# Causal attention with a gated layer and a soft mixture on one core: the score tiles of a pair's step in another order

## Chip, cores and metric

The kernel runs on one core of a Trainium2 chip. The metric is the time on the device in microseconds (us), the median over runs of the same program. The profiled execution has a time of its own and is shown beside it.

## What is computed

Three layers in a chain, the output of each being the input of the next:

```python
# attention: 4 batches x 12 heads, seq 448, head_dim 64, causal
scores = scale * q @ k.T                      # masked above the diagonal
scores = scores - scores.max(-1)
attn   = exp(scores) / (exp(scores).sum(-1) + 1e-9)
x      = attn @ v                             # -> (1792 tokens, 768)
# layer
h = x @ w_in                                  # 768 -> 2048
x = np.maximum(0.01 * h, h) @ w_out           # 2048 -> 768
# soft mixture: 8 experts, 4 slots each
logits = x @ phi                              # (1792, 32)
d = softmax(logits, over tokens); c = softmax(logits, over slots)
slot_input = d.T @ x
slot_out   = for each expert: relu(slot_input @ w1) @ w2
out = c @ slot_out
```

## The kernel before

**Tiling.** Two heads make a pair; there are 24 pairs, n = 0 to 23, six to a batch (`NP`). For each pair a step is written, in three slots, by the generator `attention_slots` (L517). Its first loop covers n = 0 to 6 and is not touched; its second loop (L563 on) covers n = 7 to 24. While a pair is attended, the score maxima of the next pair are made: a step holds the work of the pairs n - 1, n and n + 1.

**What a step makes.** The names are those of the trace; every TensorE instruction has the line of the helper that chains them, L102.
- `maxima(n + 1, tiles)` writes one or two of the four row blocks of raw scores into a tile S (block 3 is 448 columns wide, block 2 is 336, block 1 is 224, block 0 is 112, each for two heads). VectorE reads each block and head with one reduction (`junk<-S`, L372) and a short readout of 0.08 us, which give the row maxima `mxe`. `TILES` = ((3,), (0, 2), (1,)) names the three S tiles: S3, S02, S1.
- `lowering(n)` transposes the maxima (`mps`), and ScalarE spreads them into `mr` (L384).
- `weights(n, g)`, g = 0, 1, 2, writes the transposed scores minus the maxima into a tile T (T0, T1, T2; widths 448, 336, and 224 beside 112), which ScalarE turns into exponentials `P` (`P<-T`, L408). GpSimd masks and sums them (L412, L417, L421).
- `attend` multiplies `P` with v into `O`; `inverses` sums the denominators (`dn`), which ScalarE copies (L448) and VectorE inverts in two instructions (`rs`, L450); `columns` scales `O` (VectorE L483, ScalarE L484, GpSimd L485); `qk_stacks` transposes q and k of a later pair (`qkps`), read by ScalarE L349 and VectorE L350.

**The ring.** S and T tiles share one tag of two PSUM buffers and take them in turn. So each S or T tile waits for the reader of the tile two before it: VectorE's reductions if that is an S, ScalarE's exponential if it is a T.

**The rest of the work.** `stage` walks the slots. After each slot of attention TensorE gets one column of x @ w_in of the batch before: 18 matmuls into one buffer H (`up`), read by ScalarE (`g`, L669). Two of a batch's 18 slots have no column (`GAPS = (6, 15)`): the first slots of the steps n = 9, 12, 15, 18 and 21. Between these come conversions of w_in to a pair of 16-bit halves: ScalarE L200, L201, L221, L228, VectorE L203 to L205, GpSimd L222; and from about 270 us on those of w_out, with transposes `wt_ps` and products `wp_ps` on TensorE.

**Order.** TensorE's instructions are chained one after the other in the order in which the code writes them (`in_order`). On the other engines a scheduler sets the order, with attention and H ahead of conversions by a priority. Step n = 7 begins at 116.8 us, step 13 at 246.4 us, the last S tile is made in step 22, and attention ends at 502 us. What follows is H of the last batch, the logits and the experts.

Of the kernel before, what the change touches and what calls it, by code (L numbers as in the profile page):

```python
# [34 lines left out]
def tile_attn_moe_softmoe(ctx: ExitStack, tc: tile.TileContext, q, k, v, w_in, w_out, phi, w1, w2, out, dbg=None):  # L35
# [268 lines left out]
    def load_qk(n):  # L304
        b, hp = divmod(n, NP)
        t = att.tile([CP, 2, 2 * NI * D], F32, tag="qk", bufs=2, name=f"qk{n}")
        t = t.rearrange("p j (c x) -> p j c x", c=NI)
        for j, src in enumerate((q, k)):
            for a in range(2):
                nc.sync.dma_start(  # L310
                    t[:, j, :, D * a : D * (a + 1)], src[b, 2 * hp + a].rearrange("(c p) d -> p c d", p=CP)
                )
        qk_t[n] = t
        loaded_last()
# [11 lines left out]
    def reduce_v(n):  # L326

        b, hp = divmod(n, NP)
        if hp == 0:
            v_am[b] = am = const.tile([128, NP + 1], F32, tag="v_am", bufs=2, name=f"v_am{b}")  # L330
            nc.vector.memset(am, 0.0)
        with tc.issue_after(last_on(mybir.EngineType.DVE)) if b else ExitStack():
            nc.vector.tensor_reduce(v_am[b][:CP, hp : hp + 1], v_t[n], AX.XY, ALU.max, apply_absolute_value=True)

    def v_scale(b):

        am = v_am[b]
        nc.vector.tensor_reduce(am[:, NP:], am[:, :NP], AX.X, ALU.max)
        s_v[b], inv_v[b] = pow2_scale(am[:, NP:], f"v{b}")

    def qk_stacks(n):

        t = qk_t.pop(n)
        st = att.tile([128, 2, 2, S], F32R, tag="qs", bufs=2, name=f"qkt{n}")
        for j in range(2):
            p = ps_tr(f"qkps{n}_{j}", (128, S))
            for c in range(NI):
                tr(p[:, CP * c : CP * (c + 1)], t[:, j, c], ident[:CP, :CP])
            nc.scalar.copy(st[:, j, 0], p)  # L349
            nc.vector.tensor_tensor(st[:, j, 1], p, st[:, j, 0].bitcast(F32), ALU.subtract)  # L350
        st_t[n] = st

    def maxima(n, tiles):

        st = st_t[n]
        ps = psum.tile([CP, 2, 512], F32, tag="S", bufs=2, name=f"S{n}_{tiles[0]}")
        at = 0
        for i in tiles:
            w = CP * (i + 1)
            for a in range(2):  # L360
                r = slice(64 * a, 64 * a + 64)
                mm(
                    ps[:, a, at : at + w], st[r, 0, 0, CP * i : w], st[r, 1, 0, :w], start=True, stop=True,
                    skip_group_check=True,
                )
            at += w
        at = 0
        for i in tiles:
            w = CP * (i + 1)
            for a in range(2):  # L370
                junk = att.tile([CP, S], BF16, tag="junk", bufs=1, name=f"junk{n}_{i}_{a}")
                nc.vector.tensor_tensor_reduce(  # L372
                    out=junk[:, :w], in0=ps[:, a, at : at + w], in1=mask[:, S - w :], scale=-1.0, scalar=3e38,
                    op0=ALU.add, op1=ALU.min, accum_out=mxe[n % 2][:, 64 * a + i : 64 * a + i + 1],
                )
            at += w
# [9 lines left out]
    def weights(n, g):  # L386

        st, mr = st_t[n], mr_t[n].rearrange("p i c -> p (i c)")
        p = pbuf[n % 2]
        ps = psum.tile([CP, 2, 512], F32, tag="S", bufs=2, name=f"T{n}_{g}")  # L390
        at = 0
        for j in ((0,), (1,), (2, 3))[g]:
            w = S - CP * j
            for step, (kh, qh) in enumerate(((0, 0), (1, 0), (0, 1), (None, None))):
                for a in range(2):
                    r = slice(64 * a, 64 * a + 64)
                    dst = ps[:, a, at : at + w]
                    if kh is None:
                        mm(dst, onesr[r], mr[r, CP * j :], start=False, stop=True, skip_group_check=True)
                    else:  # L400
                        mm(
                            dst, st[r, 1, kh, CP * j : CP * (j + 1)], st[r, 0, qh, CP * j :], start=step == 0, stop=False,
                            skip_group_check=True,
                        )
            at += w
        x = p[g // 2][:CP].rearrange("p a j c -> p a (j c)")
        o = S if g == 1 else 0
        nc.scalar.activation(x[:, :, o : o + at], ps[:, :, :at], AF.Exp, scale=SCALE)  # L408
        if g:

            d = p[g // 2][:CP].rearrange("p a j c -> p (a j) c")[..., :CP]
            nc.gpsimd.affine_select(  # L412
                out=d, in_=d, compare_op=ALU.is_ge, fill=0.0, base=0, pattern=[[0, 4], [1, CP]], channel_multiplier=-1,
            )

        if g == 1:
            nc.gpsimd.tensor_tensor(tsum[:CP], p[0][:CP, :, 0, CP:], p[0][:CP, :, 1, : S - CP], ALU.add)  # L417
        if g == 2:
            for j in range(2):
                y = tsum[:CP, :, CP * (j + 1) :]  # L420
                nc.gpsimd.tensor_tensor(y, y, p[1][:CP, :, j, : S - CP * (j + 2)], ALU.add)  # L421
            del st_t[n], mr_t[n]
# [4 lines left out]
    def attend(n):  # L427

        p, vt = pbuf[n % 2], v_t.pop(n)
        o_t[n] = o = psum.tile([128, S], F32, tag="O", name=f"O{n}")  # L430
        for j in range(NI):
            for a in range(2):
                mm(
                    o[64 * a : 64 * a + 64, CP * j :], vt[:, a * NI + j, :], p[j // 2][:CP, a, j % 2, : S - CP * j],
                    start=j == 0, stop=j == NI - 1, skip_group_check=True,
                )
# [80 lines left out]
    def attention_slots():  # L517


        for n in range(2):  # L520
            qk_stacks(n)
            load_qk(n + 2)
            if n == 0:
                for tiles in TILES:
                    maxima(0, tiles)
        for x in range(NP):
            reduce_v(x)
        v_scale(0)
        for n in range(NP + 1):
            here, more = n < NPAIR, n + 1 < NPAIR  # L530
            if n > 0:
                attend(n - 1)
            if here:
                lowering(n)
            if more:
                maxima(n + 1, TILES[0])
            if here:
                weights(n, 0)
            yield
            if n > 0:  # L540
                inverses(n - 1)
            if more:
                maxima(n + 1, TILES[1])
            if here:
                weights(n, 1)
            yield
            if n > 0:
                columns(n - 1)
            if here:
                weights(n, 2)  # L550
            if more:
                maxima(n + 1, TILES[2])
            if n + 2 < NPAIR:
                qk_stacks(n + 2)
                if n + 4 < NPAIR:
                    load_qk(n + 4)
            if n + NP < NPAIR:
                load_v(n + NP)
            if NP <= n + NP - 1 < NPAIR:
                reduce_v(n + NP - 1)  # L560
            yield

        for n in range(NP + 1, NPAIR + 1):  # L563
            here, more = n < NPAIR, n + 1 < NPAIR
            attend(n - 1)
            inverses(n - 1)
            if here:
                lowering(n)
            yield
            if more:  # L570
                maxima(n + 1, TILES[0])
            if here:
                weights(n, 0)
            if n % NP == 1 and n + NP - 2 < NPAIR:
                v_scale(n // NP)
            yield
            columns(n - 1)
            if here:
                weights(n, 1)
            if more:  # L580
                maxima(n + 1, TILES[1])
            if here:
                weights(n, 2)
            if more:
                maxima(n + 1, TILES[2])
            if n + 2 < NPAIR:
                qk_stacks(n + 2)
                if n + 4 < NPAIR:
                    load_qk(n + 4)
            if n + NP < NPAIR:  # L590
                load_v(n + NP)
            if n + NP - 1 < NPAIR:
                reduce_v(n + NP - 1)
            yield

    TILES = ((3,), (0, 2), (1,))
    slots_of_attention = attention_slots()


# [484 lines left out]
```

## Time and profile before

| | us |
|---|---|
| median of 3 runs (lowest, highest) | 722.96 (722.45, 725.35) |
| profiled execution: its time | 725.07 |
| profiled execution: span, first to last instruction | 723.3 |
| TensorE busy in it | 603.6 (83%) |
| VectorE, ScalarE, GpSimd busy | 360.0, 290.9, 232.7 |
[...]

The profiled execution lies 2.11 us above the median. Working with its rows gives a time against 725.07; 2.11 less gives one against the median. A row of the timeline is start, duration, engine, line, operation, what it writes and reads, and in brackets how long its engine stood idle before it, with what ended that. A matmul row groups neighbouring matmuls of one shape; their ends are modelled.

### The profile page before, as it was taken

How to read it: one execution, taken by the hardware profiler on the slowest of the kernel's cores; microseconds unless marked ns; L12 is line 12 of the kernel's file. 1: busy time of each engine (PE TensorE's matmuls, PEld its weight loads, DVE VectorE, ACT ScalarE, POOL GpSimd, SP SyncE). 2: the span in 40 equal slices, each digit the busy share in tenths (PEclk: the TensorE clock that was granted, in tenths of full speed). 3: DMA queues.
4: the chain of work that ended last, by engine and by line, in shares of the span. 5: the costliest groups of instructions: out<-in, count | busy, mean ns of one | idle time of the engine just before them, and what ended most of it. 6: DMA issues, size and time to landing. Idle time of an engine off the chain costs nothing.

```text
span 723.3 us, 12309 instructions
## 1 busy us (share of the span) xinstructions
PE 603.6 (83%) x4836; PEld 342.0 (47%) x4836; DVE 360.0 (50%) x884; ACT 290.9 (40%) x571; POOL 232.7 (32%) x247
## 2 busy tenths in 40 slices
PE   3788858879889988898988978899998996998464
PEld 2465634555545545555555545454443443453124
DVE  5878646578775554464446446543646423101004
ACT  1677543466863444554435334442121112011003
POOL 4368742476763344243333233322000000000000
PEclk9999998899999988999998989999999998899968
DMA  9933163353642364463422311303989436999957
GB/s 197 251 87 77 39 188 90 108 157 90 189 145 64 105 176 139 127 185 96 108 77 79 88 47 62 93 24 118 328 318 357 157 106 241 424 423 424 424 237 305
DMA packets 102449, 125.67 MB, mean 174 GB/s; under 512 B 69240, under 2 KB 91256, under 8 KB 98296
## 3 DMA queue, kind: packets, MB, share of 16 engines
q1 hardware_dynamic: 102392, 124.89, 52.3%
q8 instruction: 38, 0.62, 0.4%
q14 instruction: 19, 0.16, 0.1%
HBM read 105.74 MB, written 19.14 MB: 173 GB/s over the span
## 4 chain that ended last, share of the span: by engine, by line
PE 52%; DVE 14%; DMA 13%; ACT 8%; POOL 6%; issue 4%; SPq 1%; DVEq 0%; ACTq 0%; POOLq 0%
PE H L102 25%; DMA w<-in_moe_w_dram 8%; PE O L102 4%; DVE junk L372 3%; PE T L102 3%; DMA raw_i_None<-in_moe_w_in_dram 3%; PE g_acc L102 3%; PE qkps L102 2%; DVE g_nat L609 2%; PE ph L942 2%; PE dn L102 2%; PE L L102 2%; DVE cv_i_None L205 2%; PE S L102 2%; POOL cv_i_None L222 2%
## 5 line engine op out<-in xcount | busy, mean ns | idle before, releaser
L102 PE MATMUL H<-x,w 128*128 128x448 f16 x1152 | 243.5, 368 | 2.1 <-ACT g L669 2.1
L102 PEld LDWEIGHTS <-w 128*128 128x128 f16 x1152 | 115.5, 103 | 122.3 <-issue 35.4
L372 DVE CUSTOM_DVE_ANT_0 junk<-S,mask 112x448 bf16<-112x448 f32 (+1 forms) x192 | 85.2, 444 | 51.2 <-PE S L102 47.7
L669 ACT ACTIVATE g<-H,iv 128x448 f32<-128x448 f32 x58 | 36.7, 632 | 120.0 <-PE H L102 104.3
L102 PE MATMUL T<-qkt 64*112 64x336 f32 (+3 forms) x576 | 60.8, 323 | 26.6 <-ACT P L408 25.9
L450 DVE RECIPROCAL rs<-rs 128x224 f32<-128x224 f32 x36 | 53.4, 1524 | 38.5 <-ACT rs L448 38.5
L408 ACT ACTIVATE P<-T 112x672 f32<-112x672 f32 (+1 forms) x72 | 56.9, 790 | 29.3 <-PE T L102 29.1
L102 PEld LDWEIGHTS T<-qkt 64*112 64x112 f32 x576 | 44.0, 183 | 37.2 <-ACT P L408 30.0
L102 PE MATMUL O<-P,v 112*64 112x448 f32 (+3 forms) x384 | 55.3, 429 | 6.3 <-POOL P L412 4.0
L412 POOL TENSOR_SCALAR_AFFINE_SELECT P<-P 112x448 f32<-112x448 f32 x48 | 31.3, 653 | 76.9 <-ACT P L408 74.2
L485 POOL TENSOR_TENSOR x<-rs,x 128x448 f16<-128x448 f32 x24 | 25.7, 1071 | 85.3 <-ACT x L484 79.9
L102 PE MATMUL S<-qkt 64*112 64x448 f32 (+1 forms) x192 | 32.6, 380 | 17.3 <-DVE mxe L372 13.7
L421 POOL TENSOR_TENSOR tsum<-tsum,P 112x448 f32<-112x448 f32 (+1 forms) x48 | 44.3, 922 | 3.3
L1030 PE MATMUL po<-w,hz 128*32 128x384 f32 x256 | 27.9, 557 | 19.1 <-DMA w<-in_moe_w_dram 19.1
L102 PEld LDWEIGHTS O<-P,v 112*64 112x64 f32 x384 | 26.5, 143 | 34.3 <-issue 16.4
L417 POOL TENSOR_TENSOR tsum<-P 112x672 f32<-112x672 f32 x24 | 40.1, 1670 | 1.5
L609 DVE STREAM_TRANSPOSE g_nat<-g 128x448 f32<-128x448 f32 x26 | 16.5, 639 | 44.0 <-ACT g L669 44.0
L350 DVE TENSOR_TENSOR qkt<-qkps,qkt 128x448 fp32r<-128x448 f32 x48 | 28.4, 619 | 18.0 <-ACT qkt L349 17.5
L934 POOL MEMSET hz<- 128x256 f32 x2 | 0.6, 311 | 108.5 <-PE g_acc L102 108.5
L102 PE MATMUL qkps<-ident,qk 112*128 112x112 f32 x192 | 31.6, 323 | 4.3 <-DMA qk<-in_q_dram 4.3
L222 POOL TENSOR_TENSOR cv_i_None<-cv_i_None,cs_i_None 128x768 f32<-128x768 f32 x16 | 26.3, 1647 | 23.7 <-ACT cs_i_None L221 23.7
L102 PE MATMUL T<-mr,onesr 64*112 64x448 f32 (+1 forms) x192 | 31.2, 321 | 2.4 <-ACT mr L384 2.4
(174 smaller groups left out, 855.7 us busy)
## 6 DMA issues: line engine op xcount, KB each, us to landing
w<-in_moe_w_dram SPq DMA_DIRECT2D x32, 1536.0 KB, 20.5
raw_i_None<-in_moe_w_in_dram SPq DMA_DIRECT2D x16, 768.0 KB, 4.8
raw_o_None<-in_moe_w_out_dram SPq DMA_DIRECT2D x10, 768.0 KB, 6.0
g_far<-g SPq DMA_DIRECT2D x32, 224.0 KB, 6.9
gb<-g_far SPq DMA_DIRECT2D x8, 896.0 KB, 6.8
wo<-wsc SPq DMA_DIRECT2D x4, 1536.0 KB, 9.7
qk<-in_q_dram SPq DMA_DIRECT2D x48, 112.0 KB, 2.4
qk<-in_k_dram SPq DMA_DIRECT2D x48, 112.0 KB, 2.7
```

The lines of the kernel that those rows point to most:

```text
L102: op(*args, **kwargs)
L222: nc.gpsimd.tensor_tensor(t, t, sg, ALU.mult)
L350: nc.vector.tensor_tensor(st[:, j, 1], p, st[:, j, 0].bitcast(F32), ALU.subtract)
L372: nc.vector.tensor_tensor_reduce(out=junk[:, :w], in0=ps[:, a, at : at + w], in1=mask[:, S - w :], scale=-1.0, scalar=3e38, op0=ALU.add, o ...
L408: nc.scalar.activation(x[:, :, o : o + at], ps[:, :, :at], AF.Exp, scale=SCALE)
L412: nc.gpsimd.affine_select(out=d, in_=d, compare_op=ALU.is_ge, fill=0.0, base=0, pattern=[[0, 4], [1, CP]], channel_multiplier=-1,)
L417: nc.gpsimd.tensor_tensor(tsum[:CP], p[0][:CP, :, 0, CP:], p[0][:CP, :, 1, : S - CP], ALU.add)
L421: nc.gpsimd.tensor_tensor(y, y, p[1][:CP, :, j, : S - CP * (j + 2)], ALU.add)
L450: nc.vector.reciprocal(rs[:, c : c + S // 2], rs[:, c : c + S // 2])
L609: nc.vector.transpose(g_nat[:, :, 32 * f : 32 * (f + n)].rearrange("p c (f x) -> p f c x", x=32), gts[b, f].rearrange("p (c x) -> p c x", ...
L669: nc.scalar.activation(g, ps, AF.Prelu, scale=iv[b][:, f : f + 1], alpha=SLOPE)
L1030: nc.tensor.matmul(po[h][32 * g : 32 * g + 32], hp[:, (t0 + t) % 8], wt[:, t, DH * h - c0 : DH * (h + 1) - c0], start=t0 + t < 4, stop=t0 ...
```

## The change

The second loop writes the same tiles in another order. Slot 2 held S3, T0 and now holds S1, T0, S3. Slot 3 held T1, S02, T2, S1 and now holds T1, T2, S02. Nothing is added or removed.

```diff
--- before.py
+++ after.py
@@ -568,21 +568,20 @@
                 lowering(n)
             yield
             if more:
-                maxima(n + 1, TILES[0])
+                maxima(n + 1, TILES[2])
             if here:
                 weights(n, 0)
+            if more:
+                maxima(n + 1, TILES[0])
             if n % NP == 1 and n + NP - 2 < NPAIR:
                 v_scale(n // NP)
             yield
             columns(n - 1)
             if here:
                 weights(n, 1)
+                weights(n, 2)
             if more:
                 maxima(n + 1, TILES[1])
-            if here:
-                weights(n, 2)
-            if more:
-                maxima(n + 1, TILES[2])
             if n + 2 < NPAIR:
                 qk_stacks(n + 2)
                 if n + 4 < NPAIR:
```

With A and B for the two buffers, and in brackets whose reader a tile waits for:
- before: S3 A (T2), T0 B (S1), T1 A (S3), S02 B (T0), T2 A (T1), S1 B (S02)
- after: S1 A (T2), T0 B (S02), S3 A (S1), T1 B (T0), T2 A (S3), S02 B (T1)

Below the diff all lines stand one lower: L669 of before is L668 of after.

On TensorE, the step of pair 21. S22_3 is the tile S3 of pair 22, T21_1 the tile T1 of pair 21; between the two pieces stand other slots' work. Before:

```order
L102 MATMUL S22_3_4635<-qkt22_4533 112x448 x2
L102 MATMUL T21_0_4642<-qkt21_4291 112x448 x6
L102 MATMUL T21_0_4642<-mr21_4622,onesr_120 112x448 x2
```

```order
L102 MATMUL T21_1_4696<-qkt21_4291 112x336 x6
L102 MATMUL T21_1_4696<-mr21_4622,onesr_120 112x336 x2
L102 MATMUL S22_0_4708<-qkt22_4533 112x112 x2
L102 MATMUL S22_0_4708<-qkt22_4533 112x336 x2
L102 MATMUL T21_2_4721<-qkt21_4291 112x224 x6
L102 MATMUL T21_2_4721<-mr21_4622,onesr_120 112x224 x2
L102 MATMUL T21_2_4721<-qkt21_4291 112x112 x6
L102 MATMUL T21_2_4721<-mr21_4622,onesr_120 112x112 x2
L102 MATMUL S22_1_4742<-qkt22_4533 112x224 x2
```

After:

```order
L102 MATMUL S22_1_4635<-qkt22_4533 112x224 x2
L102 MATMUL T21_0_4642<-qkt21_4291 112x448 x6
L102 MATMUL T21_0_4642<-mr21_4622,onesr_120 112x448 x2
L102 MATMUL S22_3_4652<-qkt22_4533 112x448 x2
```

```order
L102 MATMUL T21_1_4703<-qkt21_4291 112x336 x6
L102 MATMUL T21_1_4703<-mr21_4622,onesr_120 112x336 x2
L102 MATMUL T21_2_4715<-qkt21_4291 112x224 x6
L102 MATMUL T21_2_4715<-mr21_4622,onesr_120 112x224 x2
L102 MATMUL T21_2_4715<-qkt21_4291 112x112 x6
L102 MATMUL T21_2_4715<-mr21_4622,onesr_120 112x112 x2
L102 MATMUL S22_0_4736<-qkt22_4533 112x112 x2
L102 MATMUL S22_0_4736<-qkt22_4533 112x336 x2
```

S3 now stands behind T0 and a tile S1 ahead of it; T1 and T2 stand next to each other, and S02 closes the step.

On VectorE, the same step (the junk tiles carry pair, block and head). Before:

```order
L450 RECIPROCAL rs20_4616<-rs20_4616 128x224 x2
L372 ISA junk22_3_0_4638,mxe0_142<-S22_3_4635,mask_114 112x448
L372 ISA mxe0_142 112x1
L483 SCALAR_TENSOR_TENSOR rs20_4616<-O20_4602,v3_s_4194,rs20_4616 128x448
L372 ISA junk22_3_1_4640,mxe0_142<-S22_3_4635,mask_114 112x448
L372 ISA mxe0_142 112x1
L609 STREAM_TRANSPOSE g_nat_4110<-g2_6_4672 128x14x32
L204 TENSOR_SCALAR cv_o13_0_4683<-cv_o13_0_4683 128x384
L205 SCALAR_TENSOR_TENSOR cv_o13_0_4683<-raw_o13_0_4473,cv_o13_0_4683 128x384
```

After:

```order
L450 RECIPROCAL rs20_4616<-rs20_4616 128x224 x2
L372 ISA junk22_1_0_4638,mxe0_142<-S22_1_4635,mask_114 112x224
L372 ISA mxe0_142 112x1
L483 SCALAR_TENSOR_TENSOR rs20_4616<-O20_4602,v3_s_4201,rs20_4616 128x448
L372 ISA junk22_1_1_4640,mxe0_142<-S22_1_4635,mask_114 112x224
L372 ISA mxe0_142 112x1
L372 ISA junk22_3_0_4655,mxe0_142<-S22_3_4652,mask_114 112x448
L372 ISA mxe0_142 112x1
L372 ISA junk22_3_1_4657,mxe0_142<-S22_3_4652,mask_114 112x448
L372 ISA mxe0_142 112x1
```

The reductions of S1, which S3 waits for, stand where those of S3 stood: behind the reciprocals of pair 20 and on both sides of the scaling L483.

On ScalarE, the step of pair 8 (T8_1 and T8_2 are its tiles T1 and T2; cs_i, cv_i and w16 are conversions). Before:

```order
L221 ACTIVATE cs_i7_None_1445<-cs_i7_None_1445,w7_s_1637 128x768
L638 ACTIVATE iv0_1358<-inv_w_119,v0_s_269 128x1
L669 ACTIVATE g0_4_1691<-H0_4_1672,iv0_1358 128x448
L221 ACTIVATE cs_i8_None_1574<-cs_i8_None_1574,w8_s_1701 128x768
L638 ACTIVATE iv0_1358<-inv_w_119,v0_s_269 128x1
L408 ACTIVATE P0_448_144<-T8_1_1721 112x2x336
L228 CAST w16_1_98<-cv_i7_None_1444 128x6x128
L200 ACTIVATE cv_i9_None_1645<-raw_i9_None_1390 128x768
L201 ACTIVATE cs_i9_None_1646<-raw_i9_None_1390 128x768
L228 CAST w16_2_99<-cv_i8_None_1573 128x6x128
L201 ACTIVATE cs_i10_None_1710<-raw_i10_None_1451 128x768
L408 ACTIVATE P0_224_145<-T8_2_1746 112x2x336
```

After:

```order
L221 ACTIVATE cs_i7_None_1452<-cs_i7_None_1452,w7_s_1637 128x768
L637 ACTIVATE iv0_1358<-inv_w_119,v0_s_269 128x1
L668 ACTIVATE g0_4_1698<-H0_4_1679,iv0_1358 128x448
L228 CAST w16_1_98<-cv_i7_None_1451 128x6x128
L200 ACTIVATE cv_i9_None_1645<-raw_i9_None_1390 128x768
L201 ACTIVATE cs_i9_None_1646<-raw_i9_None_1390 128x768
L221 ACTIVATE cs_i8_None_1574<-cs_i8_None_1574,w8_s_1708 128x768
L637 ACTIVATE iv0_1358<-inv_w_119,v0_s_269 128x1
L408 ACTIVATE P0_448_144<-T8_1_1728 112x2x336
L408 ACTIVATE P0_224_145<-T8_2_1740 112x2x336
L228 CAST w16_2_99<-cv_i8_None_1573 128x6x128
L200 ACTIVATE cv_i10_None_1716<-raw_i10_None_1458 128x768
L201 ACTIVATE cs_i10_None_1717<-raw_i10_None_1458 128x768
```

The exponentials of T1 and T2 now stand together, and L228, L200 and L201, which stood behind the one of T1, stand ahead of it.

## Rows read from the trace of the kernel before

**Rows 1.** The page: busy time by engine, and the chain that ended last, by engine.

```profile
PE 603.6 (83%) x4836; PEld 342.0 (47%) x4836; DVE 360.0 (50%) x884; ACT 290.9 (40%) x571; POOL 232.7 (32%) x247
...
PE 52%; DVE 14%; DMA 13%; ACT 8%; POOL 6%; issue 4%; SPq 1%; DVEq 0%; ACTq 0%; POOLq 0%
```

**Rows 2.** Windows: length, busy PE, PEld, DVE, ACT, POOL, granted clock, DMA share, GB/s.

```profile
116.00:246.00 130.00, 112.99 (x752) 66.09 (x751) 88.89 (x220) 74.94 (x133) 71.02 (x56) 0.92 0.41 121
246.00:502.00 256.00, 228.62 (x1680) 134.72 (x1679) 128.44 (x291) 120.04 (x253) 92.05 (x89) 0.94 0.35 100
502.00:600.00 98.00, 90.05 (x777) 40.62 (x775) 46.44 (x89) 16.54 (x33) 0.00 (x0) 1.00 0.70 257
```

**Rows 3.** TensorE's waits, 116 to 246 us: total us, times, longest.

```profile
PE T L102 <- ACT P L408: 9.4, 6, 2.5
PE S L102 <- DVE mxe L372: 2.9, 2, 2.7
...
PE H L102 <- ACT g L669: 1.4, 2, 1.1
```

**Rows 4.** TensorE's waits, 246 to 502 us.

```profile
PE T L102 <- ACT P L408: 13.3, 10, 2.7
PE S L102 <- DVE mxe L372: 7.6, 9, 1.4
```

**Rows 5.** Timeline, TensorE and ScalarE, third slot of step 16: S02, T2, S1, H.

```profile
329.17 0.41 PE L102 MATMUL S<-qkt 64*112 64x112 f32 x4
...
329.38 0.73 ACT L408 ACTIVATE P<-T 112x672 f32<-112x672 f32 x1 [0.32 <-PE T L102]
...
330.16 0.57 PE L102 MATMUL T<-qkt 64*112 64x224 f32 x6 [0.58 <-ACT P L408]
...
330.92 0.26 PE L102 MATMUL T<-mr,onesr 64*112 64x112 f32 x2
...
331.38 0.35 PE L102 MATMUL S<-qkt 64*112 64x224 f32 x2 [0.20 <-DVE mxe L372]
...
332.49 3.57 PE L102 MATMUL H<-x,w 128*128 128x448 f16 x18
```

**Rows 6.** Timeline, TensorE's T2 in step 8.

```profile
149.97 0.66 PE L102 MATMUL T<-qkt 64*112 64x224 f32 x6 [1.72 <-ACT P L408]
```

**Rows 7.** Groups by line and form: busy us, mean ns of one, then idle before.

```profile
L372 DVE CUSTOM_DVE_ANT_0 junk<-S,mask 112x224 bf16<-112x224 f32 x48 | 18.6, 388 | 9.6 <-PE S L102 8.9
...
L201 ACT ACTIVATE cs_i_None<-raw_i_None 128x768 bf16<-128x768 f32 x16 | 14.4, 898 | 6.4 <-DMA raw_i_None<-in_moe_w_in_dram 4.8 <-POOL cv_i_None L222 1.6
...
L228 ACT CAST w<-cv_i_None 128x768 f16<-128x768 f32 x14 | 11.6, 830 | 1.5 <-POOL cv_i_None L222 1.4
```

**Rows 8.** Timeline, VectorE and TensorE, start of step 21: reciprocals, S3, T0, L483.

```profile
433.84 2.96 DVE L450 RECIPROCAL rs<-rs 128x224 f32<-128x224 f32 x2 [1.34 <-ACT rs L448]
...
435.39 0.46 PE L102 MATMUL S<-qkt 64*112 64x448 f32 x2
...
436.29 0.36 PE L102 MATMUL T<-mr,onesr 64*112 64x448 f32 x2
...
437.20 0.68 DVE L483 SCALAR_TENSOR_TENSOR rs<-O,v_s,rs 128x448 f32<-128x448 f32 x1
```

**Rows 9.** Timeline, VectorE: the reciprocals of step 9, and L205 in step 8.

```profile
162.51 2.96 DVE L450 RECIPROCAL rs<-rs 128x224 f32<-128x224 f32 x2 [1.42 <-ACT rs L448]
...
145.15 1.19 DVE L205 SCALAR_TENSOR_TENSOR cv_i_None<-raw_i_None,cv_i_None 128x768 int32<-128x768 int32 x1
```

**Rows 10.** Timeline, TensorE, third slot of step 14; and the window of that step.

```profile
281.55 0.57 PE L102 MATMUL T<-qkt 64*112 64x224 f32 x6 [1.04 <-ACT P L408]
...
283.88 0.53 PE L102 MATMUL S<-qkt 64*112 64x224 f32 x2 [1.30 <-DVE mxe L372]
...
285.89 5.72 PE L102 MATMUL H<-x,w 128*128 128x448 f16 x18
...
272.00:297.00 25.00, 21.50 (x156) 13.18 (x154) 9.84 (x25) 11.94 (x28) 9.60 (x8) 0.86 0.46 126
```

## Prediction

> **What bounds the kernel now.** I read the page first. TensorE is busy 83% of the span and holds 52% of the chain that ended last, VectorE 14%, ScalarE 8% [rows 1]. So time is gained where TensorE stands, and the question is for whom. The windows show that the stage the change touches, 116 to 502 us, is less dense than what follows: TensorE is busy for 113.0 of 130 us and 228.6 of 256, then for 90.1 of 98 [rows 2]. Its granted clock is 0.92 and 0.94 there, and 1.00 afterwards. The work behind 502 us waits for buffers that attention frees, and TensorE is nearly full there; I let a shift of attention's end pass on to the end one to one.
>
> Then the waits of that stage: tile T for ScalarE's exponential 9.4 + 13.3 = 22.7 us in 16 waits, and tile S for VectorE's reductions 2.9 + 7.6 = 10.5 us [rows 3, 4]. All but a little of the first is T2 waiting for the exponential of T1, once in each of the 16 steps (n = 7 to 22). All of the second is S1 waiting for the reductions of S02. Both pairs are parted by the change: T2 will wait for S3, made a slot earlier, and S1 for T2 of the step before. So **33.2 us of waits lose their place**. Three things take their place.
>
> **S02 behind T1's exponential.** S02 now takes the buffer of T1, and T2 stands between them. Step 16, where ScalarE is free, gives the size. The exponential starts at 329.38 and takes 0.73; T2 starts at 330.16, idle for 0.58 [rows 5]. Between T1 and T2 stood only S02 with 0.41. T2 lasts from 330.16 to 331.18 (S1 at 331.38 less its 0.20 of idle), 1.02 us, so with T2 in that place the buffer is free when S02 comes: nothing is left of the 0.58. Each wait shrinks by the added cover, 1.02 - 0.41 = 0.6, and the shortest of the sixteen are like step 16's. So 16 x 0.6 = 9.6 go and 22.7 - 9.6 = 13.1 stay, where ScalarE is late for reasons of its own (1.72 in step 8 [rows 6]).
>
> The order of ScalarE adds to that. In the steps 8 to 10 the conversions L228, L200 and L201 now stand ahead of T1's exponential, 0.83 + 0.90 + 0.90 = 2.6 us (L200 by the row of L201, its like) [rows 7]. If they run while TensorE still has H, they cost nothing; if they all land behind T1, 2.6 in three steps, 7.9. I take 1.2 each, 3.6, a little under the middle, since the first of them can start under H. So 16.7 stay, between 13.1 and 21.
>
> **S3 behind the reductions of S1.** This wait is new. The cover is T0. Step 21 shows the bad case, a first slot without an H column: S starts at 435.39 while VectorE's two reciprocals run from 433.84 to 436.80, and T0 ends at 436.65 [rows 8]. VectorE's list has a reduction, L483, a reduction there. A reduction of 224 takes 0.39 [rows 7], L483 0.68, the readouts lie beside what follows: 436.80 + 0.39 + 0.68 + 0.39 = 438.26, so S3 would wait 1.6. In step 9 the reciprocals end at 165.47 [rows 9], later against the first S of their step, and a wait of 2.7 comes out in the same way. The five steps 9, 12, 15, 18 and 21 give 2.7, 2.7, 1.5, 1.6 and 1.6, together 10.1. In the steps 8, 10, 11 and 22 a conversion stands among the reductions (L205 took 1.19 in step 8 [rows 9], and more in others): 1.5, 2.8, 1.9 and 0.8, together 7.0. In the other seven VectorE is free; two reductions and a readout, 0.9, lie under T0, and I put 0.15 each, 1.0. So **18.1 us of new waits**. The ends: 6, if VectorE's reciprocals come earlier as its inputs do, and 22, if each L205 is as slow as its slowest.
>
> **The clock.** In step 14 two gaps, 1.04 before T2 and 1.30 before S1, stand ahead of an H that takes 5.72; the H of step 16 takes 3.57 [rows 5, 10]. That is the half clock, 2.15 us lost, and the step's mean clock is 0.86. Over the stage the loss is at most (1 - 0.92) x 130 + (1 - 0.94) x 256 = 10.4 + 15.4 = 25.8 us [rows 2], so about ten such stretches; a slow H marks each, and step 14's stands in the rows. In the later steps, 13, 14, 20 and 22 have theirs right behind the waits that go, while in 15, 18 and 21 new waits of about 1.5 appear. I take a gain of three stretches less a little, 6.0; ahead of step 13 the new waits are as long as the old, and I take nothing. The ends: a gain of 10, or a loss of 4 x 2.15 = 8.6, if S3's waits in 12, 15, 18 and 21, which had full clock, each bring the clock down.
> [...]
>
> **What is swallowed.** Where TensorE stands behind S3 it no longer stands behind H's buffer later, 1.4 us [rows 3]. I take that off. The matmuls, DMAs and other engines' work are the same, at the same sizes: nothing.
>
> **The sum.** -33.2 + 16.7 + 18.1 - 1.4 - 6.0 = -5.8 us. Against the profiled execution 725.07 - 5.8 = 719.3; that one stood 2.11 above the median, so against the median **717**.
>
> **Rivals.**
> *The new waits bring the clock down.* The gap ahead of S3 opens in a step that has lost its H column and that ran at full clock before. If a gap of 1.3 to 1.6 us there is enough, as in step 14, four steps pay 2.15 and the gain of 6.0 is not made: -33.2 + 16.7 + 18.1 - 1.4 + 8.6 = +8.8, 731.8 against the median. It decides where a gap is as long as step 14's 1.30. For it speaks that no gap there was longer [rows 10]; against it that step 14 had two gaps close together, and S3's is one.
> *The waits simply go.* If TensorE's earlier steps bring the denominators forward too, VectorE's reciprocals are out of the way when S1 comes: S3's waits are 6 and S02's 13.1: -33.2 + 13.1 + 6 - 1.4 - 6.0 = -21.5, 701.5. For it: VectorE was busy only 128 of 256 us after 246 us [rows 2]. Against it: the reciprocals start after TensorE's `dn` in the same step, so they move with the step and not ahead of it.
> *The stage is paced by the other engines.* A step is also a ring: exponential, sums, `dn`, reciprocals, L483. Before 246 us VectorE is busy 88.9 of 130 and ScalarE 74.9. If that ring sets the step, TensorE's waits come back elsewhere and the time stays, 723. Against it: TensorE's 52% of the chain.
> *The clock stays out of it.* Then the clock's term is zero and the sum is +0.2, 723.2. For it: TensorE has 27 of these waits [rows 3, 4] and only about ten slow stretches. Against it: step 14.
> [...]
> That the order isn't what the code says can be left out: TensorE's list shows it.
>
> **How the numbers follow.** The forecast, 717 with a range of its own of 710 to 722, has 0.40; slower by the clock 0.23; the waits simply go 0.15; paced by others 0.14; clock out of it 0.08. A measurement of this kernel can tell about 0.5% from no change, 3.6 us, so faster means under 719.3 and slower over 726.6. Of the forecast 0.32 lies on the fast side, 0.07 within and 0.01 beyond. Faster 0.32 + 0.15 = 0.47; same 0.07 + 0.14 + 0.08 = 0.29; slower 0.01 + 0.23 = 0.24. The range from 703 to 731 leaves out half of the clean case and nearly half of the slow one, some 0.18.
>
> **What would show it.** In the profile after, T waits for `P` in none of the 16 steps but through S02; the waits of S for `P` come to about 17 us and the waits of S for `mxe` to about 18, the longest in the steps 9 and 12. The clock from 246 to 502 us rises to about 0.96 and stays at 0.92 before. S tiles that wait under 10 us for VectorE speak for the clean case. A clock of 0.92 or less after 246 us, with H over 5 us behind S3, speaks for the slow one. I am wrong altogether if attention's end moves and the end of the kernel doesn't, or if T2 now waits for S3's reductions.

## Result: 19.5 us faster, over three times the forecast

The changed kernel takes **704.6 us** (median of 4 runs, 703.71 to 705.66) against 724.15 of the kernel before beside it: ratio 0.9725, 95% interval 0.9685 to 0.9766. The forecast was 717, a gain of 5.8. The direction was right and 704.6 lies in the outer range, 703 to 731, but not in the forecast's own, 710 to 722.

The page of the changed kernel, busy time by engine, against [rows 1]:

```profile
PE 592.6 (84%) x4836; PEld 334.8 (48%) x4836; DVE 358.0 (51%) x884; ACT 289.7 (41%) x571; POOL 236.6 (34%) x247
```

The same 4836 matmuls keep TensorE busy for 592.6 us in place of 603.6. Nothing was taken out, so 11 us of the gain are matmuls that ran at a higher clock. The granted clock of the profiled execution, as a share of full speed, is 0.951 in the mean, against 0.932 before. In half-microsecond windows from 116 to 703 us it was 1.00 in 1063 and 0.50 in 92 of the changed kernel, 1.00 in 1005 and 0.50 in 144 of the kernel before; in the other 19 and 25 it lay between. These are the "full" and the "half" clock of the forecast; an H at 1.00 took 3.57 us.

To see where, both kernels are cut at the same work: from the first T0 matmul of step 7 to that of step 13, from there to that of step 23, and to the end. Columns as in [rows 2]; before:

```profile
117.06:246.72 129.66, 112.65 (x751) 65.94 (x748) 88.56 (x219) 74.94 (x134) 71.02 (x56) 0.92 0.42 122
246.72:481.36 234.64, 207.98 (x1530) 123.27 (x1527) 120.08 (x281) 112.49 (x238) 84.56 (x81) 0.93 0.37 104
...
481.36:723.30 241.94, 197.57 (x1848) 96.24 (x1847) 74.01 (x152) 41.12 (x85) 10.47 (x24) 0.93 0.73 289
```

After:

```profile
117.96:250.69 132.73, 113.35 (x752) 65.19 (x751) 86.63 (x219) 75.26 (x134) 73.81 (x56) 0.92 0.42 119
250.69:462.51 211.82, 194.98 (x1529) 116.31 (x1527) 119.97 (x281) 111.28 (x238) 84.58 (x81) 1.00 0.41 115
462.51:703.90 241.39, 198.00 (x1848) 96.33 (x1847) 74.04 (x152) 41.18 (x85) 10.48 (x24) 0.94 0.73 290
```

The change costs 3.1 us in the steps 7 to 12 and gives 22.8 in the steps 13 to 22; what follows stays as long as it was (241.94 and 241.39), so here the earlier start of step 23 passed on one to one. In the later steps the granted clock goes from 0.93 to **1.00**. Of the 22.8, 13.0 are busy time (207.98 to 194.98) and 9.8 idle time.

TensorE's waits, first the early stretch (117.96 to 250.69), against [rows 3]:

```profile
PE S L102 <- ACT P L408: 13.0, 7, 3.0
PE S L102 <- DVE mxe L372: 3.3, 3, 1.5
```

and the late one (250.69 to 462.51), against [rows 4]:

```profile
PE S L102 <- ACT P L408: 6.2, 6, 1.5
PE S L102 <- DVE mxe L372: 4.3, 4, 1.6
```

No T waits for `P` any more. S waits in 20 places for 26.9 us, where T and S waited for 33.2.

### The profile page after: what moved, and what is told of

It reads as the page before. It is cut to its first block, busy times and chain, and to the rows that moved or that the text cites. A ratio compares the mean times of both kernels' runs of the same rounds, so it can differ in the third digit from the quotient of the medians.

```text
span 703.9 us, 12298 instructions
## 1 busy us (share of the span) xinstructions
PE 592.6 (84%) x4836; PEld 334.8 (48%) x4836; DVE 358.0 (51%) x884; ACT 289.7 (41%) x571; POOL 236.6 (34%) x247
## 4 chain that ended last, share of the span: by engine, by line
PE 48%; DMA 13%; DVE 11%; ACT 10%; POOL 8%; issue 7%; SPq 1%; ACTq 0%; DVEq 0%; POOLq 0%
PE H L102 22%; DMA w<-in_moe_w_dram 8%; PE O L102 5%; PE g_acc L102 3%; DVE g_nat L608 2%; DVE rs L450 2%; PE S L102 2%; ACT P L408 2%; PE qkps L102 2%; POOL cv_i_None L222 2%; PE ph L941 2%; DMA raw_i_None<-in_moe_w_in_dram 2%; PE dn L102 2%; PE L L102 2%; PE T L102 2%
## 5 line engine op out<-in xcount | busy, mean ns | idle before, releaser
L102 PE MATMUL H<-x,w 128*128 128x448 f16 x1152 | 234.8, 359 | 0.7 <-ACT g L668 0.7
L102 PEld LDWEIGHTS <-w 128*128 128x128 f16 x1152 | 112.5, 100 | 113.4 <-issue 22.5
L372 DVE CUSTOM_DVE_ANT_0 junk<-S,mask 112x224 bf16<-112x224 f32 (+3 forms) x192 | 85.1, 443 | 47.8 <-PE S L102 44.7
L668 ACT ACTIVATE g<-H,iv 128x448 f32<-128x448 f32 x58 | 36.7, 633 | 112.1 <-PE H L102 101.3
L102 PE MATMUL S<-qkt 64*112 64x224 f32 (+3 forms) x192 | 33.8, 393 | 35.0 <-ACT P L408 21.8
L102 PE MATMUL O<-P,v 112*64 112x448 f32 (+3 forms) x384 | 57.4, 444 | 6.1 <-POOL P L412 4.4
L102 PE MATMUL T<-qkt 64*112 64x336 f32 (+3 forms) x576 | 58.4, 315 | 3.9 <-ACT P L408 3.2
L412 POOL TENSOR_SCALAR_AFFINE_SELECT P<-P 112x448 f32<-112x448 f32 x48 | 33.8, 708 | 82.1 <-ACT P L408 69.3
L421 POOL TENSOR_TENSOR tsum<-tsum,P 112x448 f32<-112x448 f32 (+1 forms) x48 | 46.4, 967 | 3.1
L102 PEld LDWEIGHTS S<-qkt 64*112 64x112 f32 x192 | 16.0, 184 | 50.1 <-ACT P L408 25.6
L350 DVE TENSOR_TENSOR qkt<-qkps,qkt 128x448 fp32r<-128x448 f32 x48 | 28.9, 620 | 10.5 <-ACT qkt L349 10.5
L384 ACT ACTIVATE mr<-mps,own 128x112 fp32r<-128x112 f32 x96 | 26.2, 361 | 16.0 <-PE mps L102 16.0
```

Source lines behind the costliest of these rows:

```text
L102: op(*args, **kwargs)
L372: nc.vector.tensor_tensor_reduce(out=junk[:, :w], in0=ps[:, a, at : at + w], in1=mask[:, S - w :], scale=-1.0, scalar=3e38, op0=ALU.add, o ...
L412: nc.gpsimd.affine_select(out=d, in_=d, compare_op=ALU.is_ge, fill=0.0, base=0, pattern=[[0, 4], [1, CP]], channel_multiplier=-1,)
L668: nc.scalar.activation(g, ps, AF.Prelu, scale=iv[b][:, f : f + 1], alpha=SLOPE)
```

## Experiments

Every diff is against the changed kernel; the ratios are against the kernel before, beside which each ran, and the stretches are cut at the same matmuls as above (step 7, 13, 23). The question from the first comparison was what the clock follows: two waits close together, the size of a wait, or the moment at which it falls.

### Half of the change: S1 moved up alone

```diff
                 weights(n, 1)
-                weights(n, 2)
             if more:
                 maxima(n + 1, TILES[1])
+            if here:
+                weights(n, 2)
```

> Only S1 goes ahead of T0 and S3 behind it; T1, S02, T2 keep their order. T2 keeps its wait for the exponential of T1 (22.7 us in all before), S1 loses its own (10.5), and S3 gets the one it has in the changed kernel (11.4). By waits alone the time is that of before, 724 to 725. Theory 'two gaps' (the clock falls where two waits of TensorE stand close together, as T2's and S1's did before, and a single one of about 1.5 us doesn't bring it down): most of the 15 us of lost clock from step 13 on come back, 711 to 716, clock of the late steps 0.98 or more. Theory 'one gap' (that of the prediction: each wait of 1.3 us or more costs an H at half clock): the clock stays at 0.94, 724 to 729.

Measured: 715.66 us, ratio 0.986 (0.9826 to 0.9894). The late stretch, its waits, and the place in step 13 where T2 waits for the exponential of T1:

```profile
250.39:471.15 220.76, 198.60 (x1529) 118.23 (x1527) 120.56 (x281) 111.87 (x238) 84.99 (x81) 0.98 0.39 110
...
PE T L102 <- ACT P L408: 10.8, 10, 2.2
PE S L102 <- DVE mxe L372: 3.8, 4, 1.4
...
258.61 0.56 PE L102 MATMUL T<-qkt 64*112 64x224 f32 x6 [1.80 <-ACT P L408]
```

The waits are in sum about those of the kernel before: in the early stretch 10.1 of T for `P`, 2.7 of T for `mxe` and 6.0 of S, in the late one 10.8 and 4.8, together 34.4 us against 33.2. Yet the time falls by 1.4%, some 10 us, and TensorE's busy time from step 13 to 23 from 207.98 to 198.60. So **at an equal sum of waits the clock, 0.98 in place of 0.93, is worth about 9 us**. The waits are equal only over both stretches together: in the late one, where the clock rose, they fell from 20.9 [rows 4] to 15.6, and in the early one they grew. By the time, 715.66 against 711 to 716 and 724 to 729, the "one gap" theory of the forecast is set aside: the late steps of this kernel have S3 waits of 0.5 to 1.4 and T2 waits of 0.6 to 2.2, apart from each other, and lose little. But not nothing: behind the 1.80 above, H took 4.62 in place of 3.57.

### The other half: T2 next to T1 alone

```diff
-                maxima(n + 1, TILES[2])
+                maxima(n + 1, TILES[0])
             if here:
                 weights(n, 0)
-            if more:
-                maxima(n + 1, TILES[0])
...
                 maxima(n + 1, TILES[1])
+                maxima(n + 1, TILES[2])
```

> Only T2 goes next to T1; S3 stays ahead of T0, and slot 3 is T1, T2, S02, S1. S02 waits for the exponential of T1 as in the changed kernel (15.5 us in all), and S1 for that of T2, with S02's 0.41 as its cover: about 0.45 in each of 16 steps, 7 us. Waits: -33.2 + 15.5 + 7 = -10.7 us. No S3 wait. Theory 'two gaps': S02's and S1's waits follow each other, but S1's is short; the clock gains about 10 in the late steps, 703 to 706. Theory 'one gap': the late steps keep half of their slow stretches, 708 to 713.

Measured: 703.34 us, ratio 0.9684 (0.9646 to 0.9722), as fast as the whole change or a little faster. Both stretches, and a place in step 13:

```profile
117.50:242.99 125.49, 110.08 (x750) 65.16 (x748) 87.62 (x219) 74.54 (x134) 71.47 (x56) 0.95 0.44 126
242.99:460.33 217.34, 201.40 (x1529) 119.32 (x1525) 118.56 (x281) 111.89 (x238) 84.63 (x81) 0.97 0.41 112
...
250.66 0.98 PE L102 MATMUL S<-qkt 64*112 64x112 f32 x6 [1.33 <-ACT P L408]
...
252.40 5.25 PE L102 MATMUL H<-x,w 128*128 128x448 f16 x18
```

In the early steps it is 7.2 us faster than the whole change (125.49, 132.73): S3 ahead of T0 does not wait, the waits of S are 2.4 less in sum (13.9 for 16.3), and TensorE's busy time is 3.3 less. In the late ones it is 5.5 slower, with 6.4 more busy time. The two last rows speak against the plain "two gaps" theory: one wait of 1.33, and an H of 5.25 in place of 3.57 behind it.

### The two buffers taken strictly in turn

```diff
+    turn = [0]
+
+    def ring(name):
+
+        turn[0] += 1
+        return psum.tile([CP, 2, 512], F32, tag=f"S{turn[0] % 2}", bufs=1, name=name)
...
-        ps = psum.tile([CP, 2, 512], F32, tag="S", bufs=2, name=f"S{n}_{tiles[0]}")
+        ps = ring(f"S{n}_{tiles[0]}")
...
-        ps = psum.tile([CP, 2, 512], F32, tag="S", bufs=2, name=f"T{n}_{g}")
+        ps = ring(f"T{n}_{g}")
```

The description of the kernel said that the S and T tiles take their two buffers in turn. That is not always so: S3 can get the buffer of T0. How the pool chooses was not tested. Step 12 of the changed kernel shows it, VectorE, ScalarE and TensorE:

```profile
229.50 0.39 DVE L372 CUSTOM_DVE_ANT_0 junk<-S,mask 112x224 bf16<-112x224 f32 x1 [4.38 <-PE S L102]
...
231.04 0.92 ACT L408 ACTIVATE P<-T 112x896 f32<-112x896 f32 x1 [0.55 <-PE T L102]
...
232.01 0.46 PE L102 MATMUL S<-qkt 64*112 64x448 f32 x2 [1.01 <-ACT P L408]
...
232.69 0.33 DVE L372 CUSTOM_DVE_ANT_0 junk<-S,mask 112x224 bf16<-112x224 f32 x1
```

S3 starts at 232.01, right after the exponential of T0 ends (231.96), while the second reduction of S1 comes only at 232.69, behind the reciprocals. So S3 has T0's buffer, not S1's. The same is seen in the steps 9 and 21.

> The changed kernel with two tags of one PSUM buffer each, taken strictly in turn by the S and T tiles, as the prediction had assumed; in the changed kernel the pool gave S3 the buffer of T0 in the steps 9, 12 and 21. If that is why S3 waited less there than forecast (1.71, 1.01, 1.01 in place of 2.7, 1.5 and 1.6), the three waits go to about 2.7, 2 and 1.6 and the time rises by 2 to 4 us, more where the clock falls with them. Rival: what S3 waits less is waited for behind it on VectorE; the time stays within 1 us of the changed kernel.

Measured: 711.87 us, ratio 0.9788 (0.976 to 0.9817), 4.6 us above the changed kernel by the ratios. Its waits from step 7 to 13, both its stretches, and two waits of step 9:

```profile
PE S L102 <- DVE mxe L379: 8.3, 5, 2.8
PE S L102 <- ACT P L415: 8.1, 5, 3.0
...
124.29:254.15 129.86, 111.57 (x750) 63.97 (x750) 86.96 (x219) 75.36 (x134) 73.19 (x56) 0.93 0.43 121
254.15:468.95 214.80, 196.65 (x1529) 116.74 (x1527) 119.95 (x281) 111.34 (x238) 84.70 (x81) 0.99 0.40 114
...
170.98 0.72 PE L102 MATMUL S<-qkt 64*112 64x448 f32 x2 [2.81 <-DVE mxe L379]
...
178.49 0.50 PE L102 MATMUL S<-qkt 64*112 64x112 f32 x4 [0.58 <-ACT P L415]
```

The waits came out as the prediction had priced them: 2.81, 2.08 and 1.46 in the steps 9, 12 and 21, where it had 2.7, 2.7 and 1.6 (the 1.5 for step 12 in the expectation is a slip). So the prices were near, that of step 12 somewhat high, and the buffer was wrong. But these waits cost no time: from step 7 to 23 the strict kernel takes 344.66 us and the changed one 344.55. S3 waits 3.5 us more in sum and S02 2.1 less, since it waits less behind a longer wait of S3 (0.58 in step 9, in place of 2.84). What the strict ring loses in the runs lies ahead of step 7, which it reaches at 124.29 in place of 117.96 (the kernels whose first steps are as before reach it between 115.44 and 119.96); the first seven steps, whose order is another, were tied to a strict turn too. So neither the expectation's 2 to 4 us nor its rival is borne out where it was put.

### The changed order from step 13 on

```diff
-                maxima(n + 1, TILES[2])
+                maxima(n + 1, TILES[2 if n >= 13 else 0])
             if here:
                 weights(n, 0)
-            if more:
+            if more and n >= 13:
                 maxima(n + 1, TILES[0])
...
+            if more and not (n >= 13):
+                maxima(n + 1, TILES[1])
+            if here:
                 weights(n, 2)
             if more:
-                maxima(n + 1, TILES[1])
+                maxima(n + 1, TILES[1 if n >= 13 else 2])
```

> The changed order from step 13 on, the order of before in the steps 7 to 12. By the starts of the steps the changed kernel lost 3.1 us between step 7 and step 13 and gained 22.8 from there to step 23. If each part stands for itself: 3 us less than the changed kernel, 701 to 702.5. Rival: the loss of the early steps is only shifted work of ScalarE and VectorE, which the later steps would pay in this kernel: 704 to 706.

Measured: 703.57 us, ratio 0.9706 (0.9662 to 0.9751), not to be told from the changed kernel. All its stretches:

```profile
118.22:247.70 129.48, 112.50 (x752) 65.91 (x749) 88.57 (x219) 74.88 (x134) 71.06 (x56) 0.92 0.42 122
247.70:459.23 211.53, 194.94 (x1531) 116.23 (x1529) 119.95 (x281) 111.40 (x238) 84.68 (x81) 1.00 0.41 115
...
459.23:703.60 244.37, 199.34 (x1848) 98.27 (x1847) 74.03 (x152) 41.23 (x85) 10.52 (x24) 0.92 0.72 286
```

Up to step 23 the parts add as expected: 129.48 and 211.53, 3.5 less than the changed kernel. Behind step 23 it takes 3.0 more (244.37, 241.39), of which 1.3 are busy time at a lower clock (0.92, 0.94). That last stretch, in which TensorE's order is the same in all eleven kernels, took 241.2 to 244.4 us in their profiles, so this one does not show that the gain is taken back; the measured 703.57 lies between the two ranges of the expectation.

### A longer wait of S3

```diff
-            for a in range(2):
+            for a in [0, 1] + [1, 1] * (i == 1 and n >= 14):
                 junk = att.tile([CP, S], BF16, tag="junk", bufs=1, name=f"junk{n}_{i}_{a}")
```

> The changed kernel; from step 13 on VectorE reads the second head of S1 three times in place of once, so that S3's buffer comes free 0.9 us later: a single wait of 2.3 to 2.5 in the steps 15, 18 and 21 (1.0 to 1.6 before), about 0.9 in most others, 9 us of waits in all. Theory 'size of the gap' (a single wait of 1.6 us or less leaves the clock alone, one of about 2 or more costs an H at half clock): slow H behind S3 in two or three of these steps, clock from step 13 on 0.97 to 0.98, 716 to 719. Rival 'two gaps' (a single wait never costs the clock): 1.00 there, 712 to 714.

Measured: 707.43 us, ratio 0.9716 (0.9663 to 0.9768). The late stretch and its waits:

```profile
248.56:463.90 215.34, 194.82 (x1530) 116.27 (x1528) 126.32 (x321) 111.89 (x238) 84.64 (x81) 1.00 0.40 113
...
PE S L102 <- ACT P L408: 10.0, 11, 1.4
PE S L102 <- DVE mxe L372: 5.3, 4, 1.6
```

The edit missed its aim, and 707.43 lies under both ranges of its expectation. The pool again gave S3 the buffer of T0 where that of S1 was late, and no wait grew beyond 1.62. What it made is ten S3 waits of 1.0 to 1.6 us in place of five of 0.6 to 1.6. The late stretch is 3.5 us longer, the clock stays at 1.00 and TensorE's busy time at 194.82. So **in this execution single waits of this size, in every late step, cost no clock**, which is what the forecast had feared.

### The same waits at another moment

```diff
             step = 0
+            for _ in range(9 if b == 1 and f == 0 else 0):
+                mm(ps, wq[:, 0, 0, fo : fo + 128], x16[b][:, 0, 0, :], start=True, stop=True)
```

> The changed kernel; at the start of step 13 the first matmul of one H is made nine times more (its value is overwritten), 1.8 us of busy TensorE that moves all later waits in time and changes none. Theory 'size of the gap': no slow stretch after step 13, as in the changed kernel, 706 to 707. Rival 'moment' (whether a wait of 1.3 to 1.6 us costs the clock depends on when it falls): one to three slow H in the steps 13, 15, 18, 19 or 20, 708 to 713.

Measured: 710.41 us, ratio 0.9732 (0.968 to 0.9783; the kernel before took 729.34 beside it).

```profile
115.44:249.52 134.08, 115.53 (x759) 65.86 (x759) 86.65 (x219) 75.32 (x134) 73.82 (x56) 0.92 0.42 118
249.52:462.18 212.66, 194.96 (x1531) 116.25 (x1529) 119.94 (x281) 111.44 (x238) 84.60 (x81) 1.00 0.41 115
...
146.46 0.51 PE L102 MATMUL S<-qkt 64*112 64x112 f32 x4 [3.02 <-ACT P L408]
...
147.72 5.25 PE L102 MATMUL H<-x,w 128*128 128x448 f16 x18
```

The nine matmuls lie at the seam, in the first row. In this execution the clock behind it is 1.00 and the busy time 194.96, as in the changed kernel. But it took 705.89 us, and the other three took 710.09 to 711.04, at a mean granted clock of 0.940 to 0.947 in place of 0.952: their times lie in the range of the rival. Where in them the clock was low no profile shows, and by the ratio, 0.9732, the kernel is as fast as the changed one. So the late waits leave this open. An earlier step speaks for the moment: up to step 12 this kernel's code is that of the changed kernel, and S02's wait in step 8 is 3.02 here and 3.00 there; the two last rows show an H of 5.25 behind it, where the changed kernel's took 3.57 at a granted clock of 1.00.

### A longer wait of S02

```diff
-        nc.scalar.activation(x[:, :, o : o + at], ps[:, :, :at], AF.Exp, scale=SCALE)
+        for _ in range(2 if g == 1 and n >= 13 else 1):
+            nc.scalar.activation(x[:, :, o : o + at], ps[:, :, :at], AF.Exp, scale=SCALE)
```

> The changed kernel; from step 13 on ScalarE writes the exponential of T1 twice, 0.66 us more, so that S02's single wait grows from 1.29, 0.53, 0.42, 1.45 and 1.53 us in the steps 13, 14, 15, 19 and 20 to about 1.95, 1.2, 1.1, 2.1 and 2.2, and to 0.5 in the others: 6 us more waits from step 13 to 23. Theory 'size of the gap' (single waits of about 2 us cost an H at half clock, as in the kernel with only S1 moved up, where 1.80 and 2.17 did and 1.91 didn't): slow H in two or three of the steps 13, 19 and 20, clock there 0.97 to 0.98, 221 to 223 us from step 13 to 23 in place of 211.8. Rival 'two gaps' (a single wait never costs the clock): 1.00, 217 to 219.

Measured: 720.67 us, ratio 0.991 (0.9877 to 0.9944). The late stretch, the steps 13 and 19 in it, and the wait of step 13:

```profile
246.98:472.80 225.82, 201.22 (x1529) 119.01 (x1527) 120.67 (x281) 118.81 (x248) 81.58 (x81) 0.97 0.38 108
246.98:272.60 25.62, 23.46 (x156) 13.56 (x155) 14.04 (x33) 14.79 (x28) 10.41 (x9) 0.87 0.62 179
381.28:405.80 24.52, 21.59 (x152) 12.29 (x152) 16.27 (x39) 12.60 (x28) 8.21 (x9) 0.93 0.36 91
...
255.95 0.81 PE L102 MATMUL S<-qkt 64*112 64x112 f32 x4 [2.03 <-ACT P L409]
256.69 1.75 PE L102 MATMUL qkps<-ident,qk 112*128 112x112 f32 x8
```

Here a single wait does cost the clock: behind the 2.03 the transposes `qkps` take 1.75 (0.99 in the changed kernel, at a granted clock of 1.00), and the step's clock is 0.87. S3's wait of 1.88 in step 19 has an H of 5.25 behind it and S02's of 2.43 in step 20 `qkps` of 1.58. The late stretch is 14.0 us longer than the changed kernel's, beyond both ranges; its S waits are 18.9 in place of 10.5, 8.4 more, and its busy time 6.2 more. So an edit that makes 8 us of waits costs 14, and the rival, that a single wait never costs the clock, falls.

### A mixture of the two orders

```diff
-                maxima(n + 1, TILES[2])
+                maxima(n + 1, TILES[2 if (n >= 13 and n % 3 != 0) else 0])
             if here:
                 weights(n, 0)
-            if more:
+            if more and (n >= 13 and n % 3 != 0):
                 maxima(n + 1, TILES[0])
...
                 maxima(n + 1, TILES[1])
+            if more and not (n >= 13 and n % 3 != 0):
+                maxima(n + 1, TILES[2])
```

The changed order where VectorE is free at the start of a step, and T2 alone next to T1 elsewhere: up to step 12, and in the steps 15, 18 and 21 that have no H column ahead of S3. A first form (mix) did so up to step 12 only.

> In the steps 7 to 12 only T2 next to T1 (S3, T0 then T1, T2, S02, S1), from step 13 on the changed order. By the starts of the steps the first took 125.5 us from step 7 to 13 where the changed kernel took 132.7, and the second 211.8 from 13 to 23 where the first took 217.3. If they add, 7 us less than the changed kernel: 697 to 699. If what follows attention takes back part of it (late_only began its tail 3.3 earlier and ended 0.3 earlier), 700 to 703.

> As mix, and in the steps 15, 18 and 21 too, which have no H column in their first slot, only T2 next to T1. S3 waits there 1.0 to 1.6 us for VectorE in the changed kernel and not at all where it stands ahead of T0. The steps 15, 18 and 21 took 22.1, 18.4 and 20.3 in place of 23.6, 19.5 and 20.4: 2 to 3 us less than mix, if S1's wait for the exponential of T2 costs no clock. Rival: the waits at the changes of order eat it, within 1 us of mix.

Measured: mix 703.44 us, ratio 0.9659 (0.9615 to 0.9702); mix2 **698.31 us, ratio 0.958 (0.9541 to 0.9619)**. The stretches of mix2, and its waits in the late one:

```profile
119.96:245.74 125.78, 110.45 (x750) 65.05 (x748) 87.63 (x219) 74.55 (x134) 71.45 (x56) 0.93 0.44 125
245.74:455.72 209.98, 195.10 (x1529) 116.48 (x1527) 119.71 (x281) 111.23 (x238) 84.59 (x81) 1.00 0.41 116
...
PE S L102 <- ACT P L408: 6.4, 8, 1.6
PE S L102 <- DVE mxe L372: 1.7, 2, 1.1
```

mix2 is the fastest kernel of this document, and its stretches are the sum that was looked for: the early one is as in the kernel with T2 alone, the late one 1.8 below the changed kernel, at the clock of 1.00. The times missed their ranges all the same. mix lies a little above both of its own: its stretches took 127.50 and 214.22, and in step 19 S3 waited 1.67 with an H of 5.25 behind it. mix2 lies 5.1 below mix, where 2 to 3 were expected: in the profiles its steps 15, 18 and 21 took 3.2 less, and step 19, which it does not change, 1.1 less.

## Why the prediction was right in direction and wrong in size

**The waits that go.** Right: 33.2 us lost their place, and neither T2 nor S1 waits any more.

**S02 behind T1's exponential.** Right in sum, partly by luck: 16.7 forecast, 15.5 measured (ten waits). The bad steps are 8 to 10, for the reason given, but they came to 8.8, where the forecast's own rules give about 6.2 (T2's waits there of 1.72, 0.58 and 2.03, less 0.6 each, and the 3.6), and the other thirteen to 6.7 in place of about 10.5. Step 8, ScalarE and TensorE:

```profile
145.62 0.88 ACT L200 ACTIVATE cv_i_None<-raw_i_None 128x768 f32<-128x768 f32 x1
...
146.41 0.87 ACT L201 ACTIVATE cs_i_None<-raw_i_None 128x768 bf16<-128x768 f32 x1
...
147.18 0.93 ACT L221 ACTIVATE cs_i_None<-cs_i_None,w_s 128x768 bf16<-128x768 bf16 x1
...
148.19 1.33 ACT L408 ACTIVATE P<-T 112x672 f32<-112x672 f32 x2
...
148.96 0.50 PE L102 MATMUL S<-qkt 64*112 64x112 f32 x4 [3.00 <-ACT P L408]
...
150.21 3.57 PE L102 MATMUL H<-x,w 128*128 128x448 f16 x18
```

The conversions stand ahead of the exponential, and S02 waits 3.00 us for it.

**S3 behind the reductions of S1.** Mis-sized, one of the two steps of the prediction that failed: 18.1 forecast, 11.4 measured. The five steps without a leading H came to 1.71, 1.01, 1.62, 1.44 and 1.01, 6.8 in place of 10.1: in 9, 12 and 21 the pool gave S3 the buffer of T0, and the exponential of T0 ended before VectorE's second reduction. The strict kernel shows the forecast's own numbers where that is kept from it, and shows too that it costs no time from step 7 to 23. The steps 8, 10, 11 and 22 came to 1.46, 1.47, 0.39 and 0.60, 3.9 in place of 7.0: I had put a slow L205 among the reductions of the steps 10 and 11; in step 10 it ended up behind them, and in step 11 none stood there.

**The clock.** Mis-sized, the other step that failed: a gain of 6.0 forecast, 12.3 of busy time measured (13.0 gained after step 13, 0.7 lost before). Cut at the steps, the 13.0 lie in five of them: the steps 13, 14, 19, 20 and 22 are busy for 2.8, 3.0, 2.9, 3.0 and 1.3 us less, the other five for as long as before. So the term fell short in three places. It left out step 19, which had its slow stretch in the kernel before, 2.9 us:

```profile
393.12 0.90 PE L102 MATMUL T<-qkt 64*112 64x224 f32 x6 [2.67 <-ACT P L408]
...
396.86 4.86 PE L102 MATMUL H<-x,w 128*128 128x448 f16 x18
```

It priced each of the four stretches that it named by its H alone, 2.15, together 8.6, where they gave 10.1: in step 14 the transposes `qkps` ran slow too, 1.75 in place of 0.99. And it held 2.6 of the 8.6 back, by the sentence on the steps 15, 18 and 21, that S3's waits of about 1.5 would bring the clock down as the two gaps of step 14 did, behind which it was 0.50 from 286 to 290 us. Step 14 and step 15 of the changed kernel, TensorE, against [rows 10]:

```profile
281.68 0.51 PE L102 MATMUL S<-qkt 64*112 64x112 f32 x4 [0.53 <-ACT P L408]
...
282.94 3.57 PE L102 MATMUL H<-x,w 128*128 128x448 f16 x18
...
295.23 0.46 PE L102 MATMUL S<-qkt 64*112 64x448 f32 x2 [1.62 <-DVE mxe L372]
...
295.62 3.58 PE L102 MATMUL H<-x,w 128*128 128x448 f16 x18
```

S3 waits 1.62 in step 15, longer than either gap of step 14 before, and H behind it takes 3.58, at a granted clock of 1.00. The argument against the slow rival, that step 14 had two gaps close together and S3's is one, named the right outcome. But the trace of before could not carry it either: its step 15 has gaps of 0.94 and 1.31, as close as those of step 14, and an H of 3.57 behind them.

**What is swallowed.** Right: H's wait for its buffer went from 2.1 to 0.7 in the whole run, 1.4.

**The sum again**, from step 7 to 23: -33.2 + 15.5 + 11.4 - 1.4 - 12.3 = -20.0, and the stretches give 364.30 - 344.55 = 19.75. So the account is closed with the terms that the prediction named; two of them were mis-sized, S3's by 6.7 and the clock's by 6.3, and both the same way.

**The rivals.** "The waits simply go" named 701.5, near the result, but not by its own way: S3's waits were not 6 and S02's not 13.1, and the clock made up for it. The slow rival had the wrong sign of the clock. "Paced by the others" fell: step 23 began 18.9 us earlier. "The clock stays out of it" fell with the granted clock of 1.00 in place of 0.93, and with the kernel that moved S1 alone, 10 us faster at an equal sum of waits. No run here shows its term of zero: the term came to 12.3 us of busy time, and a single wait of 2.03 was followed by `qkps` of 1.75 in place of 0.99.

**What stays open.** What exactly brings the clock down. Waits and what stands behind them, late steps:

| kernel, step | waits, us | behind them, us (mean granted clock in it, before and changed) |
|---|---|---|
| before, 14 | 1.04 and 1.30 | H 5.72 (0.62) |
| before, 15 | 0.94 and 1.31 | H 3.57 (1.00) |
| before, 20 | 2.63 and 1.02 | H 5.69 (0.62) |
| changed, 15 and 18 | 1.62; 1.44 | H 3.58 (1.00); H 3.58 (1.00) |
| S1 alone, 13 | 1.80 | H 4.62 |
| S1 alone, 19 | 1.91 | H 3.57 |
| T2 alone, 13 | 1.33 | H 5.25 |
| mix, 19 | 1.67 | H 5.25 |
| longer wait of S02, 13 | 2.03 | `qkps` 1.75 (0.99 in the changed kernel) |

So neither "two gaps" nor "size of the gap" holds as a rule. In the late steps the single waits of 2.03 and 2.43 us (longer wait of S02), 2.17 (S1 alone) and 2.67 (before, step 19) all had slow matmuls behind them; from 1.3 to 1.9 the runs show both answers: the changed kernel's waits of 1.44, 1.45, 1.53 and 1.62 had an H of 3.57 or 3.58 behind them, while 1.33, 1.67, 1.80 and 1.88 in other kernels had one of 4.62 or 5.25. In step 8 the same wait of 3.0 had an H of 3.57 behind it in the changed kernel and of 5.25 in the one with the nine matmuls. So the moment at which a wait falls stays the rival that no run here rules out. Of the single waits named here only those over 2 us were followed by slow matmuls every time in the late steps, and that is all the runs say.

## To carry to other kernels

Here the waits that went were worth more than their length, since TensorE's clock went from 0.93 to 1.00 in the same stretch: from step 13 to 23, 9.8 us of idle time and 13.0 of busy time. So look at the matmuls behind a wait and add what they run longer. Put the tile whose reader is slow where another tile's work stands between it and the next user of its buffer, and decide that step by step: of the four orders here the changed one was the best in the late steps and the worst in the early ones. Where a pool deals buffers, read from the trace which engine a tile really waited for before pricing a ring by hand.

## What the runs showed of the hardware

- At equal sums of waits (34.4 and 33.2 us) two kernels differed by 10 us, and TensorE's busy time for the same matmuls differed by 9 from step 13 to 23, at granted clocks of 0.98 and 0.93.
- Ten S3 waits of 1.0 to 1.6 us left the granted clock at 1.00 for 215 us; in another kernel, with waits of 1.88, 2.03 and 2.43 us among its own, it was 0.97 over 226 us, with 6.2 us more busy time than in the changed kernel.
- The same wait in the same step, 3.00 and 3.02 us in two kernels of the same code up to there, had an H of 3.57 us behind it in one and of 5.25 in the other.
